# Exact 12-bit-part products from the first unit of the second batch on, in a fused sketch attention and SwiGLU kernel

## The chip, the cores and the metric

The kernel runs on one core of a Trainium2 chip. The metric is the device time of one execution in microseconds (us). Five engines work side by side, each through its own queue in order: TensorE (PE, with its weight loads shown as PEld), VectorE (DVE), ScalarE (ACT), GpSimd (POOL) and SyncE (SP), which issues most of the DMAs.

## The reference

There are 4 batches of 4 heads, 1088 positions and 32 channels. Queries and keys are projected by two 8 x 32 sketches, and the outer product of the two projections gives 64 features per position. The attention is linear: sums over the keys, then one quotient per query. Its output, 4352 tokens of 128 channels, goes through a SwiGLU block with 1536 hidden channels.

```python
def phi(x):
    a = np.einsum('rd,bhsd->bhsr', S1, x)
    b = np.einsum('rd,bhsd->bhsr', S2, x)
    return np.einsum('bhsi,bhsj->bhsij', a, b).reshape(*x.shape[:-1], r * r)
kv = np.einsum('bhsf,bhsd->bhfd', k_p, v);  z = np.sum(k_p, axis=2)
num = np.einsum('bhsf,bhfd->bhsd', q_p, kv)
den = np.einsum('bhsf,bhf->bhs', q_p, z)[..., None] + 1e-06
x = (num / den)                       # regrouped to (tokens, 128)
g = x @ w_gate;  silu = g * (1.0 / (1.0 + np.exp(-g)))
out = (silu * (x @ w_val)) @ w_out
```

The sketches and the three weights come as 64-bit floats and are narrowed to fp32 in the kernel.

## The kernel before, in words

**The SwiGLU work.** Each batch is cut into three blocks of tokens, of 384, 384 and 320. The hidden channels are cut into 12 chunks of 128. A *unit* (i, j) is the gate and the value product of block i with chunk j, the SiLU, and the product of the two, which goes to a slot of hbuf. A *down* (L936) multiplies such a slot with w_out and adds to the block's accumulator, a PSUM bank called acc. Batch 0 is handled by a loop over z (30 units, after six that are written out by hand). Then all downs of batch 0 that are left run in a row. Batches 1 to 3 are one loop over y = 0 to 107 (L1177), nine blocks of 12 units: y 0 to 35 is batch 1, y 36 to 71 batch 2, the rest batch 3. After each unit one down runs, which lags some units behind.

**Two kinds of products.** A plain unit (L903) makes both products in fp32: two matmul instructions each. A cut unit (L868) makes the value product, or with both=True both products, of fp32r parts that are exact in few bits. The weights are cut into w1, wb and wd (L835), the tokens into x1, x0 and xd (L850). A cut product is wd.xd in one bank (L877), and w1.x1 + wb.x0 in another (L883, L884). ScalarE scales the first into a tile called sum (L889). VectorE adds the second from PSUM to it (scalar_tensor_tensor, L892). In a cut unit the last product, SiLU times value, runs on GpSimd (L901); in a plain unit it runs on VectorE (L928). Cutting a token block takes one ScalarE pass (L858), a difference (L859) and a VectorE pass (L863). The plain units are y < 38; y 38 to 47 cut the value product; from y = 48 on both are cut; y = 107 is plain. The value weights are cut at y 2 to 21, the gate weights at y 14 to 33, with differences and wd on GpSimd (L838).

**The attention of the next batches** is a generator, attentions (L563). parts_of (L1087) advances it a step or two after each unit; group (L1093) runs it up to the next yield "pe", and then does the TensorE work behind it. Most of its steps are VectorE instructions: features (L355), transposes (L305, L540), the denominators (L719 to L741), the features of the queries (L355) and their transposes phT (L750). The TensorE work is numerators (L760, matmuls L770, copies into xT L787), values (L674, matmuls L366 and L678), which needs the feature sums zs that GpSimd adds up (L521), and the sketches (L332, L320). spread_out (L683) then issues six DMAs and the loads of the next values. The groups stand at y = 12, 36 and 60. The group at 12 does the last two thirds of batch 1's numerators and the values and sketches of batch 2.

**PSUM** has eight banks. Up to y = 36, units take turns over three of them (g0, g1, g2). After that, bank() (L110) hands out the bank that was touched longest ago among seven, without acc and without those that a group holds.

**Order.** Every engine runs its instructions in the order in which this code issues them. A matmul waits for its inputs and for its bank's last reader, and nothing behind it on TensorE passes it.

Of the kernel before, what the change touches and what calls it, by code (L numbers as in the profile page):

```python
# [19 lines left out]
def kernel(  # L20
# [265 lines left out]
    def run(*gens):  # L286
        for g in gens:
            for _ in g:
                pass
# [231 lines left out]
    def feature_sums(phk):  # L521

        rows = phk[:].rearrange("p c h i j -> p c (h i j)")
        s = apool.tile([P, 4, H * F], FP32, tag="zs", name="zs")
        add = lambda o, a, b: nc.gpsimd.tensor_tensor(out=o, in0=a, in1=b, op=ALU.add)  # L525
        add(s[:], rows[:, 0:4, :], rows[:, 4:8, :])
        add(s[:, 0:2, :], s[:, 0:2, :], s[:, 2:4, :])
        add(s[:, 0, :], s[:, 0, :], s[:, 1, :])
        add(s[:, 0, :], s[:, 0, :], rows[:, 8, :])
        return s[:, 0, :]  # L530

    def turns(b):

# [29 lines left out]
    def attentions():  # L563

        yield from turns(1)
        hold("a", "b")
        kp, qp = wide("a"), wide("b")
        for ps, products in ((kp, key_products), (qp, query_sketches)):
            for i, c in enumerate(kpieces):
                products(ps[:, i, :], *c)
        ka = apool.tile([P, NC * H, R], FP32, tag="kas", name="kas")
        qab = apool.tile([P, 2, NC * H, R], FP32, tag="qab", name="qab", bufs=2)
        fac = None, qab  # L580

        def sketch(ps, i):
            c0, c1 = kpieces[i]
            return ps[:, i, 0 : 64 * (c1 - c0)].rearrange("p (x t r) -> p x t r", t=2, r=R)

        for i, (c0, c1) in enumerate(kpieces):
            nc.scalar.copy(ka[:, H * c0 : H * c1, :], sketch(kp, i)[:, :, 0, :])
        phk = apool.tile([P, NC, H, R, R], FP32, tag="phk", name="phk")
        for n, (i, c0, c1) in enumerate(((0, 0, 3), (0, 3, 5), (1, 5, 7), (1, 7, 9))):
            first = H * (c0 - kpieces[i][0])  # L590
            kb = sketch(kp, i)[:, first : first + H * (c1 - c0), 1, :]
            key_features(phk, (ka[:, H * c0 : H * c1, :], kb), c0, c1)
            if n < 2:
                q0, q1 = kpieces[n]
                nc.scalar.copy(
                    qab[:, :, H * q0 : H * q1, :], sketch(qp, n).rearrange("p x t r -> p t x r")
                )
            if n == 1:
                release("b")
            if n == 3:  # L600
                release("a")
            if n % 3 != 1:
                yield
        zs = feature_sums(phk)
        for i, _ in enumerate(turns(2)):
            if i % 2:
                yield
        hold("a", "b")
        kvz = wide("a")
        values(kvz[:, 0, :], phk, zs)  # L610
        kq = wide("b")
        fac2, copies = sketches([
            (0, NC - 1, kq[:, 0], kq[:, 1]),
            (NC - 1, NC, kvz[:, 1, 0 : 2 * F], kvz[:, 1, 2 * F : 4 * F]),
        ])
        spread = spread_out(1, kvz[:, 0, :])
        for _ in range(4):
            yield
            run_copies(copies, 1)
        release("a", "b")  # L620
        step = query_step(1, fac, spread)
        yield from step(0, 3)
        numerators(1, spread, 0, 3)
        yield "first"
        yield from step(3, NC)
        phk = hbuf[:, NH - 6 :, :].rearrange("p s (n h i j) -> p (s n) h i j", h=1, i=R, j=R)
        phk = phk.rearrange("p (c h) o i j -> p c (h o) i j", h=H)
        yield from features(phk, fac2, ())
        zs = feature_sums(phk)
        yield from turns(3)  # L630
        yield "pe"
        numerators(1, spread, 3, NC)
        hold("a", "b")
        kv = bank()
        values(kv, phk, zs)
        kp, qp = wide("a"), wide("b")
        fac3, copies = sketches([(c0, c1, kp[:, i], qp[:, i]) for i, (c0, c1) in enumerate(kpieces)])
        spread = spread_out(2, kv)
        run_copies(copies, 2)
        yield  # L640
        run_copies(copies, 2)
        release("a", "b")
        yield
        yield from features(phk, fac3, ())
        zs = feature_sums(phk)
        yield from query_step(2, fac2, spread)(0, NC)
        yield "pe"
        numerators(2, spread, 0, NC)
        kv = bank()
        values(kv, phk, zs)  # L650
        spread = spread_out(3, kv)
        for _ in range(4):
            yield
        yield from query_step(3, fac3, spread)(0, NC)
        yield "pe"
        numerators(3, spread, 0, NC)
        yield

    def run_copies(copies, n):
        for f, *args in copies[:n]:  # L660
            f(*args)
        del copies[:n]
# [132 lines left out]

    LAG = 2
    hidden = {}
    acc = {}  # L800
    todo = []
# [14 lines left out]
    def whole(ap):  # L816
        return ap.bitcast(FP32)
# [14 lines left out]
                for k in range(2):  # L832
                    yield [x[:, k] for x in t]

    def cut_weights(w, at, steps):  # L835

        def put(at, f, **args):
            steps.setdefault(at, []).append(lambda: f(**args))  # L838

        for c, (w1, wb, wd) in enumerate(homes(w)):  # L840
            src = w[:, 3 * c : 3 * c + 3, :]
            low = fpool.tile([P, 3, P], FP32, tag="sgl", name="low", bufs=6)[:]
            w_parts[id(w), c] = (w1, wb, wd)
            sub = dict(op=ALU.subtract)
            put(at + c, nc.scalar.activation, out=w1, in_=src, func=AF.Copy, scale=CUT)
            put(at + 4 + c, nc.gpsimd.tensor_tensor, out=low, in0=src, in1=whole(w1), **sub)
            put(at + 12 + c, nc.scalar.activation, out=wb, in_=low, func=AF.Copy, scale=BETA)
            put(at + 16 + c, nc.gpsimd.tensor_tensor, out=wd, in0=whole(w1), in1=whole(wb), **sub)

    def cut_tokens(i, engine=nc.gpsimd):  # L850

# [16 lines left out]
    def cut_unit(i, j, both=False):  # L868
# [22 lines left out]
        for p, s in zip(ps, sums):  # L891
            nc.vector.scalar_tensor_tensor(  # L892
                out=s, in0=p, scalar=1.0 + 1.0 / BETA, in1=s, op0=ALU.mult, op1=ALU.add
            )
        sg = fpool.tile([P, BW], FP32, tag="sg", name="sg", bufs=3)[:, 0:n]
        nc.scalar.activation(sg, sums[0] if both else g, AF.Silu)  # L896
        slot_of[i, j] = slots.pop(0)
        hj = hbuf[:, slot_of[i, j], :]
# [4 lines left out]
    def unit(i, j, late=False, between=(None, None)):  # L903
# [4 lines left out]
        for o, w in ((g, wg), (u, wv)):  # L908
# [3 lines left out]
                o[:, 0:n], w[:, j, :], xT[:, t0 : t0 + n], start=True, stop=True  # L912
            )
        sg = fpool.tile(
            [P, BW], FP32, tag="sgl" if late else "sg", name="sg", bufs=6 if late else 3
        )
        nc.scalar.activation(sg[:, 0:n], g[:, 0:n], AF.Silu)  # L917
        slot_of[i, j] = slots.pop(0)
# [163 lines left out]


    att = attentions()
    ahead = [None]

    def parts_of(n):  # L1087

        for _ in range(n):
            if ahead[0] not in ("pe", "end"):  # L1090
                ahead[0] = next(att, "end")

    def group():  # L1093
        while ahead[0] != "pe":
# [45 lines left out]
    for z, (i, j) in enumerate(seq):  # L1140
        if z == 17:
            free_banks.pop()
            turn[0] %= 4
        unit(i, j)
        for p in parts.get(z, ()):
            part(*p)
        if z in (24, 25, 26):
            catch_up()
        if z == 6:
            load_k(1)  # L1150
            load_v(1, [nc.sync] * 4)
            load_q(1)
        if z >= 17:
            todo.remove(order[0])
            todo.insert(0, order.pop(0))
            down()
        if z >= 17:
            parts_of(1)
    todo.sort()
    while todo:  # L1160
        for _ in range(min(3, len(todo))):
            down()
        if ahead[0] != "first":
            parts_of(1)
    while ahead[0] != "first":
        parts_of(1)

    slots[:] = range(NH - 6)

    line = [3 * b + k for b in range(1, B) for k in ((0, 2, 1) if b == B - 1 else range(3))]
    END = len(line) * NCH
    PLAIN, VALUE = 3 * NCH + 2, 4 * NCH
    coming_x = iter(())
    cutting = {}
    for y in range(END):  # L1177
        i, j = line[y // NCH], y % NCH
        if y in (NCH, 3 * NCH, 5 * NCH):
            group()  # L1180
        if y == 3 * NCH:
            oldest[0] = True
            hold("acc")
            run(cut_tokens(i, nc.vector))
        if y < PLAIN or y == END - 1:
            unit(i, j)
        else:
            cut_unit(i, j, both=y >= VALUE)
        lag = LAG if y < PLAIN else min(5, END - y + 1)
        for _ in range(2):  # L1190
            if len(todo) > lag:
                down()
        parts_of(2 if y in (0, 4, 6, 7, 8) else 1)
        for w, at in ((wv, 2), (wg, 14)):
            if y == at:
                cut_weights(w, at, cutting)
        for step in cutting.pop(y, ()):
            step()
        if j == 4 and 3 * NCH < y < END - NCH:
            coming_x = cut_tokens(line[y // NCH + 1])  # L1200
        if j in (4, 6):
            next(coming_x, None)
    ps = wide("a")[:, 0, 0:D]
    for j in range(NCH):
        if todo and j % 4 == 0:
# [40 lines left out]
```

## Time and profile before

| what | value |
|---|---|
| 8 runs, median (lowest to highest) | 292.91 us (292.09 to 293.52) |
| the profiled execution's own time | 292.41 us |
| its span from first to last instruction | 290.7 us |
| around the span | 1.7 us |
| granted TensorE clock | 1.00 in the whole span |
| batch 0's last unit ends, downs in a row | 77.35 to 92.6 us |
| y = 0 starts | 92.6 us |
| numerators of the groups at y = 12, 36, 60 start | 114.6, 163.0, 206.8 us |
| L892, L889, L901 (cut units) | 526, 465, 1016 ns each |
| L928, L917 (plain units) | 524, 474 ns each |
| L525 (feature sums) on 128x1024, 128x512, 128x256 | 2362, 1470, 729 ns each |

The profile lists for each engine its busy time, and for each group of equal instructions the number, the mean duration and what the engine waited for. A matmul's end is modelled, so the distance from one start to the next on TensorE says more than the duration. The chain of waits lists the work that led to the end, in order of time: start, duration, what ran. The timeline lists instructions of an engine with the idle time before them in brackets.

### The profile page before, as it was taken

How to read it: one execution, taken by the hardware profiler on the slowest of the kernel's cores; microseconds unless marked ns; L12 is line 12 of the kernel's file. 1: busy time of each engine (PE TensorE's matmuls, PEld its weight loads, DVE VectorE, ACT ScalarE, POOL GpSimd, SP SyncE). 2: the span in 40 equal slices, each digit the busy share in tenths (PEclk: the TensorE clock that was granted, in tenths of full speed). 3: DMA queues.
4: the chain of work that ended last, by engine and by line, in shares of the span. 5: the costliest groups of instructions: out<-in, count | busy, mean ns of one | idle time of the engine just before them, and what ended most of it. 6: DMA issues, size and time to landing. Idle time of an engine off the chain costs nothing.

```text
span 290.7 us, 6170 instructions
## 1 busy us (share of the span) xinstructions
PE 283.9 (98%) x2307; PEld 204.3 (70%) x2307; DVE 200.8 (69%) x400; ACT 154.6 (53%) x369; POOL 130.2 (45%) x144
## 2 busy tenths in 40 slices
PE   7899999999999999999999999999999999999995
PEld 7545566667666555755667677778788988888985
DVE  3997988875542997188893369997567675676651
ACT  3567565431301432353243365578688888888860
POOL 3215322138000308029741039676466676576660
PEclk9999999999999999999999999999999999999999
DMA  6564292315511100140010020001001010020101
GB/s 198 153 213 110 64 302 82 99 59 162 118 16 27 17 0 2 36 102 0 0 28 3 2 50 0 2 0 27 2 1 28 2 23 0 0 32 0 24 2 27
DMA packets 26142, 14.63 MB, mean 50 GB/s; under 512 B 18688, under 2 KB 24192, under 8 KB 26112
## 3 DMA queue, kind: packets, MB, share of 16 engines
q1 hardware_dynamic: 25456, 14.13, 19.3%
q8 instruction: 18, 0.29, 0.4%
q10 hardware_dynamic: 656, 0.10, 0.2%
q14 instruction: 12, 0.10, 0.1%
HBM read 11.41 MB, written 2.23 MB: 47 GB/s over the span
## 4 chain that ended last, share of the span: by engine, by line
PE 91%; DVE 3%; DMA 1%; issue 1%; ACT 1%; POOL 0%; SPq 0%; DVEq 0%
PE PS L911 32%; PE PS L942 28%; PE PS L877 7%; PE PS L883 7%; PE PS L884 7%; PE PS L879 2%; PE PS L770 2%; PE PS L332 2%; PE PS L366 2%; DMA kld<-in_k_dram 1%; PE PS L320 1%; DVE sum L892 1%; PE PS L957 1%; PE PS L475 1%; PE PS L423 1%
## 5 line engine op out<-in xcount | busy, mean ns | idle before, releaser
L942 PE MATMUL PS<-hbuf,wo 128*128 128x384 f32 (+2 forms) x288 | 104.7, 460 | 0.4 <-DVE o L971 0.4
L901 POOL TENSOR_TENSOR hbuf<-sg,sum 128x384 f32<-128x384 f32 (+1 forms) x69 | 69.9, 1016 | 53.6 <-ACT sg L896 31.3
L892 DVE SCALAR_TENSOR_TENSOR sum<-PS,sum 128x384 f32<-128x384 f32 (+1 forms) x128 | 62.6, 526 | 29.5 <-ACT sum L889 27.2
L917 ACT ACTIVATE sg<-PS 128x384 f32<-128x384 f32 (+1 forms) x75 | 35.4, 474 | 68.5 <-PE PS L911 66.1
L942 PEld LDWEIGHTS PS<-hbuf,wo 128*128 128x128 f32 x288 | 52.5, 189 | 17.6 <-issue 0.7
L911 PE MATMUL PS<-xT,wg 128*128 128x384 f32 (+1 forms) x150 | 59.1, 476 | 0.0
L911 PE MATMUL PS<-xT,wv 128*128 128x384 f32 (+1 forms) x150 | 58.2, 470 | 0.2 <-DVE wv L270 0.2
L889 ACT ACTIVATE sum<-PS 128x384 f32<-128x384 f32 (+1 forms) x128 | 53.4, 465 | 5.6 <-PE PS L877 5.2
L928 DVE TENSOR_TENSOR hbuf<-sg,PS 128x384 f32<-128x384 f32 (+1 forms) x69 | 36.1, 524 | 28.6 <-PE PS L911 26.8
L911 PEld LDWEIGHTS PS<-xT,wv 128*128 128x128 f32 x150 | 28.2, 190 | 18.0 <-DVE hbuf L928 0.9
L911 PEld LDWEIGHTS PS<-xT,wg 128*128 128x128 f32 x150 | 27.6, 190 | 18.2 <-issue 1.2
L896 ACT ACTIVATE sg<-sum 128x384 f32<-128x384 f32 (+1 forms) x59 | 29.7, 503 | 17.1 <-DVE sum L892 16.4
L877 PE MATMUL PS<-xd,gphq 128*128 128x384 f32 (+1 forms) x59 | 34.6, 587 | 0.0
L883 PE MATMUL PS<-x,w 128*128 128x384 f32 (+1 forms) x69 | 25.4, 368 | 0.0
L877 PE MATMUL PS<-xd,wd 128*128 128x384 f32 (+1 forms) x69 | 24.6, 357 | 0.0
L884 PE MATMUL PS<-x,wb 128*128 128x384 f32 (+1 forms) x69 | 22.6, 328 | 0.0
L883 PE MATMUL PS<-x,graw 128*128 128x384 f32 (+1 forms) x59 | 19.2, 325 | 0.0
L884 PE MATMUL PS<-x,graw 128*128 128x384 f32 (+1 forms) x59 | 19.1, 324 | 0.0
L877 PEld LDWEIGHTS PS<-xd,wd 128*128 128x128 f32 x69 | 13.1, 189 | 6.8
L838 POOL TENSOR_TENSOR low<-wv,w 128x384 f32<-128x384 f32 x4 | 4.7, 1175 | 25.4 <-ACT w L838 25.4
L877 PEld LDWEIGHTS PS<-xd,gphq 128*128 128x128 f32 x59 | 11.1, 189 | 6.4 <-issue 0.4
L525 POOL TENSOR_TENSOR zs<-hbuf 128x1024 f32<-128x1024 f32 x2 | 4.7, 2362 | 21.5 <-PE PS L911 11.7
(129 smaller groups left out, 339.9 us busy)
## 6 DMA issues: line engine op xcount, KB each, us to landing
kld<-in_k_dram SPq DMA_DIRECT2D x4, 544.0 KB, 4.3
vld<-in_v_dram SPq DMA_DIRECT2D x12, 144.0 KB, 5.4
qld<-in_q_dram SPq DMA_DIRECT2D x3, 544.0 KB, 4.3
raw<-in_moe_w_out_dram SPq DMA_DIRECT2D x4, 384.0 KB, 4.1
out_dram<-o SPq DMA_DIRECT2D x28, 48.0 KB, 1.9
raw<-in_moe_w_gate_dram SPq DMA_DIRECT2D x3, 384.0 KB, 3.3
raw<-in_moe_w_val_dram SPq DMA_DIRECT2D x3, 384.0 KB, 3.3
out_dram<-o SPq DMA_DIRECT2D x16, 40.0 KB, 1.7
```

Source lines behind the costliest of these rows:

```text
L332: nc.tensor.matmul(ps[32 * a : 32 * a + 64, 64 * (c - c0) : 64 * (c - c0) + 64], kT[:, c, a : a + 2, :].rearrange("p a t -> p (a t)"), s12 ...
L877: nc.tensor.matmul(d, wd, xd, start=True, stop=True)
L883: nc.tensor.matmul(p, w1, x1, start=True, stop=False)
L884: nc.tensor.matmul(p, wb, x0, start=False, stop=True)
L889: nc.scalar.activation(s, d, AF.Copy, scale=-1.0 / BETA)
L892: nc.vector.scalar_tensor_tensor(out=s, in0=p, scalar=1.0 + 1.0 / BETA, in1=s, op0=ALU.mult, op1=ALU.add)
L896: nc.scalar.activation(sg, sums[0] if both else g, AF.Silu)
L901: nc.gpsimd.tensor_tensor(out=hj[:, 0:n], in0=sg, in1=sums[-1], op=ALU.mult)
L911: nc.tensor.matmul(o[:, 0:n], w[:, j, :], xT[:, t0 : t0 + n], start=True, stop=True)
L917: nc.scalar.activation(sg[:, 0:n], g[:, 0:n], AF.Silu)
L928: nc.vector.tensor_tensor(out=hj[:, 0:n], in0=sg[:, 0:n], in1=u[:, 0:n], op=ALU.mult)
L942: nc.tensor.matmul(acc[i][:, 0:n], wo[:, j, :], hidden[i, j][:, 0:n], start=(j == 0), stop=(j == NCH - 1),)
```

## The change

1. **Units.** All units y 0 to 106 are cut: the value product alone for y < 31, both from y = 31 on (GATES). The downs lag five units in all three batches. The rotation over seven banks begins at y = 0.
2. **Value weights** are cut in batch 0's loop, z = 24 to 29, with the differences on VectorE (z = 27). The first token block is cut during the row of downs, on VectorE; the differences of blocks 2 and 4 of the nine are on VectorE too.
3. **Gate weights** are cut from y = 8 to 28, the differences on VectorE; the tiles for them are four slots of hbuf, so the loop starts with 17 slots and not 21.
4. **Groups** stand at y = 7, 16, 34 and 64. The numerators of batch 1's last two thirds become a group of their own (y = 7), values and sketches of batch 2 follow at y = 16.
5. **Attention steps** run ahead in the row of downs: two at a time, and on after the first numerators ("turned", begun). From y = 36 on one step per two units. The feature sums of batches 2 and 3 are five GpSimd adds, spread over four steps of what runs beside them. The four copies of the sketches run in one go.

```diff
     def feature_sums(phk):
-        add(s[:], rows[:, 0:4, :], rows[:, 4:8, :])
-        add(s[:, 0:2, :], s[:, 0:2, :], s[:, 2:4, :])
-        add(s[:, 0, :], s[:, 0, :], s[:, 1, :])
-        add(s[:, 0, :], s[:, 0, :], rows[:, 8, :])
-        return s[:, 0, :]
+        def last():
+            add(s[:, 0, :], s[:, 0, :], s[:, 1, :])
+            add(s[:, 0, :], s[:, 0, :], rows[:, 8, :])
+        return s[:, 0, :], [
+            lambda: add(s[:, 0:2, :], rows[:, 0:2, :], rows[:, 4:6, :]),
+            lambda: add(s[:, 2:4, :], rows[:, 2:4, :], rows[:, 6:8, :]),
+            lambda: add(s[:, 0:2, :], s[:, 0:2, :], s[:, 2:4, :]),
+            last,
+        ]
+    def beside(gen, steps):
+        for x in gen:
+            if steps:
+                steps.pop(0)()
+            yield x
...
         yield from step(0, 3)
+        yield "turned"
         numerators(1, spread, 0, 3)
         yield "first"
         yield from step(3, NC)
+        yield "pe"
+        numerators(1, spread, 3, NC)
+        yield
...
-        zs = feature_sums(phk)
-        yield from turns(3)
+        zs, sums = feature_sums(phk)
+        yield from beside(turns(3), sums)
         yield "pe"
-        numerators(1, spread, 3, NC)
...
-        run_copies(copies, 2)
-        yield
-        run_copies(copies, 2)
+        run_copies(copies, 4)
...
+    def take(steps, n):
+        for _ in range(n):
+            if steps:
+                f, args = steps.pop(0)
+                f(**args)
...
+        if z == 24:
+            lows = [fpool.tile([P, 3, P], FP32, tag="sgl", name="low", bufs=6)[:] for c in range(4)]
+            first, low, second, third = cut_weights(wv, [(nc.vector, low) for low in lows])
+        if z in (25, 26):
+            take(first, 2)
+        if z == 27:
+            take(low, 4)
+        if z > 27:
+            take(second, 2)
+            take(third, 2)
...
-        if ahead[0] != "first":
-            parts_of(1)
-    while ahead[0] != "first":
+        if begun[0]:
+            x_steps = x_steps or cut_tokens(HEAD, nc.vector)
+            next(x_steps, None)
+        parts_of(1 if begun[0] or ahead[0] == "turned" else 2)
+    while not begun[0]:
         parts_of(1)
-    slots[:] = range(NH - 6)
+    run(x_steps or cut_tokens(HEAD, nc.vector))
+    slots[:] = range(NH - 10)
...
-    PLAIN, VALUE = 3 * NCH + 2, 4 * NCH
+    GROUPS, GATES = (7, 16, 34, 64), 31
+    for m, i in enumerate(line[1:], 1):
+        gen = cut_tokens(i, nc.vector if m in (1, 3) else nc.gpsimd)
+        for at in {1: (8, 9), 3: (34, 35), 6: (65, 69)}.get(m, (NCH * m - 9, NCH * m - 4)):
+            token_steps.setdefault(at, []).append(gen)
+    oldest[0] = True
+    hold("acc")
+    lows = [hbuf[:, NH - 10 + c, :].rearrange("p (c f) -> p c f", f=P) for c in range(4)]
     for y in range(END):
-        if y in (NCH, 3 * NCH, 5 * NCH):
+        if y in GROUPS:
             group()
-        if y < PLAIN or y == END - 1:
+        if y == END - 1:
             unit(i, j)
         else:
-            cut_unit(i, j, both=y >= VALUE)
-        lag = LAG if y < PLAIN else min(5, END - y + 1)
+            cut_unit(i, j, both=y >= GATES)
-        parts_of(2 if y in (0, 4, 6, 7, 8) else 1)
+        parts_of(y < 36 or y % 2)
+        if y == 8:
+            gate_rows = cut_weights(wg, [(nc.vector, low) for low in lows])
+        for n, row in enumerate(gate_rows):
+            if y >= (8, 12, 16, 22)[n] and (n < 3 or y % 2 == 0):
+                take(row, 1)
+        for gen in token_steps.get(y, ()):
+            next(gen, None)
```

cut_weights returns its four rows of steps (w1, difference, wb, wd) instead of placing them by unit; the tiles sg have five buffers instead of three.

## The prediction

> **What bounds the kernel now.** I read the page's busy row and slices first, then the chain of waits, then the VectorE and GpSimd timelines at the places where the change puts work.
>
> ```profile
> PE 283.9 (98%) x2307; PEld 204.3 (70%) x2307; DVE 200.8 (69%) x400; ACT 154.6 (53%) x369; POOL 130.2 (45%) x144
> ...
> DVE  3997988875542997188893369997567675676651
> ...
> POOL 3215322138000308029741039676466676576660
> PEclk9999999999999999999999999999999999999999
> ...
> PE 91%; DVE 3%; DMA 1%; issue 1%; ACT 1%; POOL 0%; SPq 0%; DVEq 0%
> ```
>
> TensorE works all the time at full clock and makes 91% of the chain, so its instruction stream is the time. VectorE is the next limit: in slices 14 to 21 (about 92 to 152 us, batch 1) it is mostly at 7 to 9 tenths, where GpSimd is nearly idle until 128 us.
>
> The price of a unit is the distance between two downs (L942) in the chain of waits.
>
> ```profile
> 100.45 0.65 PE PS L942 x2
> 101.10 1.29 PE PS L911 x4
> 102.39 0.65 PE PS L942 x2
> ...
> 157.57 0.54 PE PS L942 x2
> 158.11 1.08 PE PS L911 x4
> 159.19 0.54 PE PS L942 x2
> ...
> 177.87 0.65 PE PS L942 x2
> ...
> 179.68 0.65 PE PS L942 x2
> ...
> 199.37 0.65 PE PS L942 x2
> ...
> 201.06 0.65 PE PS L942 x2
> ...
> 220.40 0.54 PE PS L942 x2
> ...
> 221.81 0.54 PE PS L942 x2
> ```
>
> At 384 tokens: plain 1.94 us, value product cut 1.81, both cut 1.69. At 320: plain 1.62, both 1.41. The value-only unit at 320 is not in the trace; it lies between 1.62 and 1.41, and I take the middle, 1.52.
>
> **What TensorE saves.**
> - y 0 to 23, plain to value-only at 384: 24 x 0.125 = 3.0 us (exact periods over runs of units: 1.935 and 1.813, so 2.9).
> - y 24 to 30, the same at 320: 7 x 0.10 = 0.7 (bounds 0 and 1.4).
> - y 31 to 35, plain to both at 320: 5 x 0.20 = 1.0.
> - y 36 and 37, plain to both at 384: 2 x 0.25 = 0.5.
> - y 38 to 47, value-only to both at 384: 10 x 0.12 = 1.2.
>
> Together 6.3 us, between 5.6 and 7.0. The downs, numerators, values and sketches have the same matmuls as before, in another order.
>
> **What moves to the other engines.** The instruction order of the changed program shows 107 cut units against 69. A value-only unit costs VectorE what a plain one did (L892 526 ns for L928 524), ScalarE one L889 more (465 ns, at 53% busy) and GpSimd one L901 (1.0 us per 1.8 us). GpSimd takes that easily by itself. VectorE gets in batch 1 what it did not have: four gate differences and two token differences (0.56 each, by L859) and three xd passes (L863, 0.5 to 0.6), some 5 us in 70. The weight differences at z = 27 fall into idle time (VectorE waits 3.2 us before 74.0). They push the following steps by some 0.6 us; the first numerators are reached by TensorE after 13 downs, at 85.6, and phT would be ready near 83.8, because the output transpose that VectorE waits 4.0 us for at 85.1 now stands behind it. Eleven downs (5.9 us) then cover cutting the first token block (ScalarE 0.5, VectorE 0.6 and 0.6, and a 0.95 us product between them): ready near 89.9, needed at 92.5. I cost the start of batch 1 at nothing; without this cover it would be those 2.7 us.
>
> **What TensorE will wait for.** I laid the VectorE order of the new program against the units' times above, with spacings from the timeline (768-element passes 0.86 to 0.99, L892 0.47, the denominators 2.35 in all).
> - *Group at y = 7.* TensorE arrives after seven units without and two downs, 92.5 + 9.5 = 102.0. VectorE has seven L892 (3.3), five transposes and passes of step(3, NC) and the denominators, 10.1 us in all and first work at 92.6: phT near 102, banks free near 102.8. Wait 0.9 (bounds 0 and 2).
> - *Group at y = 16.* The sums are five adds between the hidden products of y 10 to 13: 3 x 1.35 + 2 x 0.75 = 5.5 us (1.35 is the undisturbed spacing of the 128x512 add at 112.2 in GpSimd's timeline) more in units that give GpSimd 7.3 us and take 4 of it. zs ends some 11.3 us after y = 10's products, and the ones-product needs it at 10.6. With a collision, 0.8 (0 to 2). In exchange the 0.46 us hole at 119.2, where TensorE waits in the sketches, goes.
> - *Batch 1's end.* From y = 26 on the denominators, and then a query feature pass (L355) or a phT pass per unit of 1.4 to 1.6 us, put VectorE about 1 us behind. The output transpose of block 4 and the group at y = 34 then come late: 0.6 (0 to 1.5).
> - *y = 36.* Before, the group at 36 cut its block at once, and two plain units covered it:
>
> ```profile
> 165.88 0.53 ACT L858 ACTIVATE x<-xT 128x384 fp32r<-128x384 f32 x1
> 166.44 0.56 DVE L859 TENSOR_TENSOR x<-xT,x 128x384 fp32r<-128x384 f32 x1 [0.17 <-ACT x L858]
> 167.04 0.56 DVE L863 SCALAR_TENSOR_TENSOR xd<-x,x 128x384 fp32r<-128x384 f32 x1
> ```
>
> Now the difference is issued after unit 34 and xd after unit 35, behind both of its L892. These cannot start before unit 35's last product, 0.54 us before unit 36; the pair takes 0.93, xd 0.56, so xd is at least 0.9 us late, and the first matmul of unit 36 is wd.xd. With ScalarE's queue (x1 stands between the copies of units 34 and 35) I get 1.4 (0.9 to 2).
> - *y = 52, 53.* The denominators of batch 3 (2.35) now stand ahead of unit 52's L892 pair and the output transpose that frees acc. By the units' period that is 1.0 late (0 to 1.5). Before, the same wait stood at 195.0, with 0.62 in front of L942; that one goes.
>
> Waits added 4.7, gone 1.1: 3.6 net. Nothing queued behind these waits can pass, on TensorE, so they count in full. SP only gets the spread and value loads of batch 2 four units later; its reader L719 stands four units behind the group, 7.3 us against 6 x 0.6 of issues and a landing like the one before 77.9, which was 2.5 behind its last issue.
>
> Sum: 6.3 - 3.6 = 2.7 us less. From the profiled 292.41 (span 290.7 and 1.7 around it) that is 289.7; the median of the runs is 0.5 higher, and I forecast for it 290.0, between the two readings 289.7 and 290.2.
>
> **The shared port.** The row that speaks against the change is this one, VectorE's first product of batch 3 and what GpSimd did then:
>
> ```profile
> 129.75 2.07 DVE L719 TENSOR_TENSOR phq<-spread,qab 128x768 f32<-128x768 f32 x1
> ...
> 133.62 0.95 DVE L719 TENSOR_TENSOR phq<-spread,qab 128x768 f32<-128x768 f32 x1
> ```
>
> ```profile
> 128.65 2.36 POOL L525 TENSOR_TENSOR zs<-hbuf 128x1024 f32<-128x1024 f32 x1 [11.68 <-PE PS L911]
> 131.08 2.68 POOL L525 TENSOR_TENSOR zs<-zs 128x512 f32<-128x512 f32 x2
> ```
>
> The first one took 1.1 us more than the second, and it ends 0.8 to 0.9 us (its normal length) after GpSimd's add. L892, which reads one input from PSUM, keeps its 0.55 us throughout. The Trainium skill, in "SBUF — State Buffer", in the section that tells engine ports from DMA ports, says that a VectorE instruction with two SBUF inputs and a GpSimd instruction exclude each other for the whole instruction, whoever is first. By that rule, each such VectorE instruction in batch 1 waits up to the whole GpSimd instruction that it meets; for 25 of them at 1.0 us it would be 25 us of VectorE time, and the change a loss. The trace is milder: nine L719 average 1159 ns over a median of 951, 0.2 us each, and nine L355 (phq) 1023 over 942, 0.1 each. My waits hold 0.2 to 0.3 for some of them.
>
> **The rivals.**
> 1. *Clean* (0.17). The waits are covered by the banks' slack, because every short wait lets VectorE catch up: then 6.3 less, and some of the 1.1 gone too. For it: before, VectorE at 9 tenths in slices 14, 15 and 17 to 21 stalled TensorE only at groups. Against: the wait at y = 36 is forced. 286.0 to 287.6.
> 2. *Eaten* (0.17). The five waits each reach their upper bound, 9.0 instead of 4.7: gain 6.3 - 7.9 = -1.6; half of the way there is 291.5 to 293.5, of which I give 0.10 to still faster and 0.07 to no change.
> 3. *Slower* (0.13): the port between VectorE and GpSimd. Between y = 0 and 33 VectorE gets 25 instructions with two SBUF inputs (L719, L355, L741, the differences), all now beside a GpSimd that works half the time or more: 4 up to y = 6, where VectorE has no slack, 9 up to y = 15 with 4.3 us of slack (13.3 us of work in 17.6), 12 up to y = 33 with 3.5 (26.5 in 30). At 0.55 each (half an L901): 2.2 + 0.7 + 3.1 = 6.0 more, and 295 to 296. It decides from about 0.42 each (1.7 + 0 + 1.5 = 3.2, which eats the 2.7). For it: between 129 and 152 us, where GpSimd was busy, eight such instructions lost 1.1, 0, 0.4, 0.1, 0.3, 0, 0 and 0.8, 0.33 on average. Against: the averages above.
> 4. That the change doesn't do what it says is excluded by the order: the units and groups stand where the text puts them.
>
> **How the numbers follow.** The forecast's case, 287.6 to 291.5, has 0.53. Its own bounds come from the waits: 0.9 (only the forced one) gives 286.5, all upper ones 294. Faster by over 0.2% (0.6 us, about what a measurement of this kernel can tell from no change): 0.53 + 0.17 + 0.10 = 0.80; within: 0.07; slower: 0.13. The range leaves out the slower case and most of no change, and the low end of the clean one: 286.4 to 292.6.
>
> **What would show it.** Right: down-to-down distances of 1.81 in y 6 to 15 and of 1.69 from y = 36; idle TensorE in front of L786 (numerators) near 102, and 0.9 to 2 in front of the first wd.xd of unit 36; VectorE above 8 tenths in batch 1. Wrong: L735 or L355 averaging over 1.4 us (rival 3); value-only units longer than 1.85; a wait of several us in front of the ones-product at y = 16; or none at y = 36.

## The result: slower by 1.5%

The changed kernel takes 296.8 us (median of 11 runs, 296.2 to 298.3), the kernel before 292.77 (32 runs, 292.08 to 293.52). The ratio is 1.0154, with a 95% interval of 1.0140 to 1.0167. The forecast was a faster kernel, 290.0 (286.4 to 292.6). The changed kernel's times lie at two levels: 296.2 to 296.8 where the granted clock is 0.998 or more, and 298.0 to 298.3 where it is 0.992 to 0.994. The profiled execution (298.18, span 296.4) is of the second; the half clock, below, makes the levels.

The page of the changed kernel: the busy row, three rows of slices, the chain's shares.

```profile
PE 282.3 (95%) x2362; PEld 211.9 (71%) x2362; DVE 218.3 (74%) x430; ACT 179.8 (61%) x427; POOL 165.8 (56%) x178
...
DVE  3997988873967879359996578898866666576651
...
POOL 3216322156601858938999367656647675666660
PEclk9999999999999999989999999999999999999999
...
PE 77%; POOL 9%; DVE 6%; issue 4%; DMA 1%; ACT 1%; SPq 0%; POOLq 0%; ACTq 0%; DVEq 0%
```

TensorE fell from 98% to 95% busy and from 91% to 77% of the chain. GpSimd, which had 0% of the chain, has 9%: in slice 17 (119 to 126 us) and slices 19 to 22 (133 to 163 us) it is nearly full. The waits of TensorE from 92 us on say where (us in total, times, longest):

```profile
PE PS L694 <- POOL zs L525: 2.0, 1, 2.0
PE PS L906 <- DVE xd L892: 1.7, 1, 1.7
PE PS L971 <- DVE o L1000: 1.3, 1, 1.3
PE PS L906 <- POOL gphq L877: 1.2, 2, 1.0
PE PS L786 <- DVE phT L766: 1.0, 1, 1.0
PE PS L971 <- POOL hbuf L930: 0.9, 1, 0.9
```

(L694 is the ones-product, L906 wd.xd, L971 the down, L786 the numerators.) The kernel before had 0.7 there in all. As distances between matmul starts beyond the matmul's own length, which are a little longer, the waits are: y = 16 2.23 (ones-product); y = 28 to 33 1.03, 1.13 and 0.42 (down, and wd.xd for the gate weights); y = 36 1.82; y = 52 and 53 1.50 (in front of the down behind unit 53); y = 64 1.17.

The account of the profiled execution: by the units' periods TensorE's work is 6.3 us less, yet the span is 5.7 longer (296.4 against 290.7), so 12.0 went elsewhere. Found are 9.3 in these seven waits, less 1.1 that the kernel before had; 1.6 at half clock behind the first of them; 0.5 in the numerators at y = 34 (1.94 against 1.48 in the chains of waits; I read it as PSUM banks that came free late, which is not shown); 0.6 with those at y = 7 (2.16 from the down ahead of them to the matmul behind them, where the same numerators took 1.59 before). That is 10.9. Of the other 1.1, 0.3 stand in front of a down at 178.3 us and 0.4 lie in y 72 to 107 (55.80 against 55.36 us), with no single wait to name; the rest I can't place.

**The half clock.** TensorE's timeline of the changed kernel, and its windows (busy times, then the granted clock):

```profile
123.72 0.32 PE L694 MATMUL PS<-zs,ones 128*32 128x64 f32 x8 [2.04 <-POOL zs L525]
...
125.29 2.15 PE L320 MATMUL PS<-s,qT 128*32 128x64 f32 x72
```

```profile
120.50:125.00 4.50, 2.46 (x115) 2.21 (x116) 1.08 (x3) 0.39 (x2) 4.42 (x6) 1.00 0.01 4
125.00:128.40 3.40, 3.40 (x84) 2.91 (x79) 0.00 (x0) 1.73 (x5) 1.42 (x2) 0.50 0.16 39
128.40:135.00 6.60, 6.60 (x28) 4.69 (x26) 5.58 (x8) 4.90 (x12) 2.33 (x2) 1.00 0.58 129
```

After 2.04 us without work the clock is 0.50 for 3.4 us, which costs about half of that: the 1.6 us between the levels. The idle time of 1.7 us at y = 36 has no such sequel.

### The profile page after: what moved, and what is told of

Read it like the earlier page. It is cut to its first block, busy times and chain, and to the rows that moved or that the text cites. A ratio compares the mean times of both kernels' runs of the same rounds, so it can differ in the third digit from the quotient of the medians.

```text
span 296.4 us, 6492 instructions
## 1 busy us (share of the span) xinstructions
PE 282.3 (95%) x2362; PEld 211.9 (71%) x2362; DVE 218.3 (74%) x430; ACT 179.8 (61%) x427; POOL 165.8 (56%) x178
## 3 DMA queue, kind: packets, MB, share of 16 engines
HBM read 11.41 MB, written 2.23 MB: 46 GB/s over the span
## 4 chain that ended last, share of the span: by engine, by line
PE 77%; POOL 9%; DVE 6%; issue 4%; DMA 1%; ACT 1%; SPq 0%; POOLq 0%; ACTq 0%; DVEq 0%
PE PS L971 24%; PE PS L940 15%; PE PS L906 9%; PE PS L912 8%; PE PS L913 8%; POOL hbuf L930 4%; POOL zs L525 4%; PE PS L908 3%; PE PS L786 2%; DVE sum L921 2%; PE PS L332 2%; DMA kld<-in_k_dram 1%; PE PS L320 1%; PE PS L366 1%; PE PS L986 1%
## 5 line engine op out<-in xcount | busy, mean ns | idle before, releaser
L930 POOL TENSOR_TENSOR hbuf<-sg,sum 128x384 f32<-128x384 f32 (+1 forms) x107 | 113.3, 1064 | 72.8 <-ACT sg L925 46.4
L921 DVE SCALAR_TENSOR_TENSOR sum<-PS,sum 128x384 f32<-128x384 f32 (+1 forms) x183 | 89.8, 525 | 38.3 <-ACT sum L918 30.2
L971 PE MATMUL PS<-hbuf,wo 128*128 128x384 f32 (+2 forms) x288 | 105.0, 461 | 2.4 <-DVE o L1000 1.3
L918 ACT ACTIVATE sum<-PS 128x384 f32<-128x384 f32 (+1 forms) x183 | 77.7, 467 | 20.6 <-PE PS L906 18.9
L971 PEld LDWEIGHTS PS<-hbuf,wo 128*128 128x128 f32 x288 | 51.4, 188 | 12.3 <-issue 2.3
L906 PE MATMUL PS<-xd,gphq 128*128 128x384 f32 (+1 forms) x76 | 44.1, 580 | 2.9 <-DVE xd L892 1.7
L912 PE MATMUL PS<-x,w 128*128 128x384 f32 (+1 forms) x107 | 43.6, 407 | 0.0
L906 PE MATMUL PS<-xd,wd 128*128 128x384 f32 (+1 forms) x107 | 42.6, 398 | 0.0
L946 ACT ACTIVATE sg<-PS 128x384 f32<-128x384 f32 (+1 forms) x37 | 17.4, 474 | 21.2 <-PE PS L940 19.6
L940 PE MATMUL PS<-xT,wv 128*128 128x384 f32 (+1 forms) x74 | 28.8, 471 | 0.2 <-DVE wv L270 0.2
L906 PEld LDWEIGHTS PS<-xd,wd 128*128 128x128 f32 x107 | 20.4, 190 | 10.9 <-issue 0.4
L957 DVE TENSOR_TENSOR hbuf<-sg,PS 128x384 f32<-128x384 f32 (+1 forms) x31 | 16.2, 524 | 10.0 <-PE PS L940 9.5
L912 PEld LDWEIGHTS PS<-x,w 128*128 128x128 f32 x107 | 20.2, 188 | 4.1 <-ACT xT L803 0.3
L906 PEld LDWEIGHTS PS<-xd,gphq 128*128 128x128 f32 x76 | 14.3, 189 | 12.2 <-POOL gphq L877 2.2
L913 PEld LDWEIGHTS PS<-x,wb 128*128 128x128 f32 x107 | 20.1, 188 | 3.7
```

The costliest lines, as they stand in the source:

```text
L906: nc.tensor.matmul(d, wd, xd, start=True, stop=True)
L912: nc.tensor.matmul(p, w1, x1, start=True, stop=False)
L913: nc.tensor.matmul(p, wb, x0, start=False, stop=True)
L918: nc.scalar.activation(s, d, AF.Copy, scale=-1.0 / BETA)
L921: nc.vector.scalar_tensor_tensor(out=s, in0=p, scalar=1.0 + 1.0 / BETA, in1=s, op0=ALU.mult, op1=ALU.add)
L930: nc.gpsimd.tensor_tensor(out=hj[:, 0:n], in0=sg, in1=sums[-1], op=ALU.mult)
```

## The experiments

First theory: GpSimd's queue makes the waits from y = 16 to 33, and four orders of VectorE's work (token parts, denominators, phT, banks) those from y = 34 on. Rival: VectorE, or its port shared with GpSimd, makes them all. The kernels ran in four groups, each beside the kernel before (medians 292.6 to 292.7). "Waits" are the distances defined above.

**The sums together** (295.39, 295.22 to 295.48; ratio 1.0091, 1.0074 to 1.0108; clock 1.0)

```
-        yield from beside(turns(3), sums)
+        for f in sums:
+            f()
+        yield from turns(3)
```

and the same beside query_step(2, ...).

> The feature sums of batches 2 and 3 are issued in one go ahead of the turns and query steps, not spread between GpSimd's hidden products; nothing else differs from the changed kernel. If GpSimd's queue order holds TensorE up at y = 16 (wait of 2.0 us in front of the ones-product, then 3.4 us at half clock), the wait and the half clock go: 2.2 + 1.7 us less than the profiled 298.2, so 294 to 295 us, and the waits at y = 28 to 33 stay (2.6 us) because GpSimd has the same work. If VectorE is what is late (rival), the ones-product was waiting for features, not for the adds behind hidden products, and the time stays at 296 to 298.

The wait in front of the ones-product goes. In the sketches behind it 0.79 are left, where the kernel before had 0.46 and the forecast had counted on none. No half clock follows: 1.4 us under the median, 1.1 under the executions at full clock, and 0.4 above the range that was expected. At y = 25 to 33 2.7 us of waits stay (0.74 of them now name VectorE's output transpose), so the spread of the sums is not what makes those.

**The wait filled** with 20 useless matmuls of 256 columns ahead of the ones-product (297.11, 296.87 to 297.81; ratio 1.0153, 1.0136 to 1.017; clock 0.999 to 1.0)

```
+        if begun[0] and not warmed:
+            warmed.append(1)
+            keep_warm(20, 256, ps=kv[:, 256:512])
...
+    warmed = []
```

> Twenty matmuls of 256 columns without a use (about 2.1 us at full clock) are put between the value products and the ones-product of the group at y = 16, in unused columns of the same bank. If the half clock behind that group comes from TensorE's idle 2 us, the granted clock stays 1.00 and every run is at the lower of the two levels of the changed kernel, 296.2 to 296.8 (the upper one is 298.0 to 298.3). If the clock drops for another reason, the two levels stay, or the time grows by up to 2 us.

No execution has the half clock, and y 16 to 23 take 14.32 us where the changed kernel's profile has 14.80. The time is 0.3 above the range that was expected; y = 0 begins 1.2 us later in this profile, which I can't explain. So it is idleness that brings the half clock (by four executions here; the last section counts all), and filling it without ending the wait gains nothing at the median.

**Block 3's token parts at y = 34** (296.75, 295.18 to 296.9; ratio 1.0124, 1.0097 to 1.0152)

```
+        if y == 34:
+            run(token_steps.pop(34)[0])
+            token_steps.pop(35)
```

> The block of y = 36 is cut at once in the group at y = 34, ahead of unit 34, not in two steps behind units 34 and 35. If the wait of 1.8 us in front of the first product of unit 36 comes from VectorE's order (the step of the forecast), it goes and the time falls by 1.5 to 1.8 us. If VectorE is simply late there, or the wait only moves into unit 34 (its sums stand behind the cut), it falls by less than 0.7.

The wait of 1.82 at y = 36 goes, but one of 0.83 comes in front of a down at 175.7. At equal clock the gain is 1.3 (295.18 against 296.5 at full clock, 296.8 against 298.1 at the lower), between the theory's 1.5 to 1.8 and the rival's 0.7.

**Plain units up to y = 23** (294.86, 294.48 to 295.16; ratio 1.0071, 1.0056 to 1.0086; clock 1.0)

```
-        if y == END - 1:
+        if y < 24 or y == END - 1:
```

> Units y = 0 to 23 are plain, as before the change; the rest of the change stays. TensorE's products cost 24 x 0.12 = 2.9 us more, and GpSimd loses 24 hidden products (24 us of its queue). If GpSimd is the bound up to y = 33, the waits at y = 16 and y = 28 to 33 (2.2 and 2.6 us) and the half clock (1.7 in the profiled run) go: net 1.9 to 3.6 us less than the changed kernel. If VectorE is the bound, its work is the same (a product for a sum), the waits stay and the time is 1 to 3 us more.

All waits that name GpSimd go, at y = 16 as at 28 to 33, and the half clock; those at y = 36, 53 and 64 stay at 1.82, 1.50 and 1.17. Although TensorE has 3.0 us more to do, the time is 1.9 less. The next runs turned to y 34 to 64.

**One attention step per unit** from y = 36 on too (298.42, 298.3 to 299.75; ratio 1.0206, 1.0177 to 1.0235)

```
-        parts_of(y < 36 or y % 2)
+        parts_of(1)
```

> The changed kernel with one attention step per unit from y = 36 on too, where the changed kernel takes one per two units. Theory of the late orders: the 1.17 us in front of the group at y = 64 goes (phT is ready units earlier), the 1.50 at y = 52 and 53 stays or moves with its denominators, the waits at y = 16, 28 to 33 and 36 stay: 295.0 to 296.5. Rival (VectorE itself is short of time from y = 36 on, so the pace is not what makes phT late): waits of the same 1.2 us or more come back in front of other units of y 36 to 60, and the time stays at 296.5 or rises.

The wait at y = 64 goes as the theory said, but new ones of 0.70, 0.53 and 1.16 come between 176 and 189 us and the one of 1.50 behind unit 53 is still 1.20: the rival. VectorE is busy 24.81 of the 25 us from 170 to 195.

**One part alone, in the kernel before:** the gates cut from y = 38 on (296.29, 296.02 to 296.39; ratio 1.0121, 1.0101 to 1.0141; clock 1.0)

```
-    PLAIN, VALUE = 3 * NCH + 2, 4 * NCH
+    PLAIN, VALUE = 3 * NCH + 2, 3 * NCH + 2
```

> The kernel before with one part of the change alone: the gate weights cut from y = 38 on instead of y = 48; plain units, sums, groups and numerators as before. Ten units at 1.69 instead of 1.81 us are 1.2 us less TensorE time. Theory (the TensorE savings are right, and what eats them is GpSimd in y 10 to 33 and four late orders): 291.4 to 291.9, the whole 1.2 or nearly. Rival (cut gates cost more than their periods show, by the port between VectorE's xd and GpSimd): 292.5 or more, with waits in front of units of y 38 to 47.

Here my theory of late orders fell. Ten units get 0.12 us shorter on TensorE each, no order is touched, and the kernel is 3.7 us slower. VectorE's timeline, first in the kernel before and then in this one, tells why:

```profile
178.76 1.29 DVE L719 TENSOR_TENSOR phq<-spread,qab 128x768 f32<-128x768 f32 x1
179.97 0.55 DVE L892 SCALAR_TENSOR_TENSOR sum<-PS,sum 128x384 f32<-128x384 f32 x1
180.43 0.94 DVE L726 TENSOR_REDUCE dot<-phq 128x96 f32<-128x768 f32 x1
181.60 0.56 DVE L892 SCALAR_TENSOR_TENSOR sum<-PS,sum 128x384 f32<-128x384 f32 x1 [0.23 <-PE PS L884]
```

```profile
182.38 1.01 DVE L892 SCALAR_TENSOR_TENSOR sum<-PS,sum 128x384 f32<-128x384 f32 x2
183.32 0.94 DVE L726 TENSOR_REDUCE dot<-phq 128x96 f32<-128x768 f32 x1
184.18 1.00 DVE L892 SCALAR_TENSOR_TENSOR sum<-PS,sum 128x384 f32<-128x384 f32 x2
185.10 0.44 DVE L735 TENSOR_TENSOR dot<-dot,qab 128x288 f32<-128x288 f32 x1
```

In the first, the unit's sum takes 0.46 us (179.97 to 180.43) and the step beside it 0.94, 1.40 of a period of 1.81, and VectorE idles 0.23. In the second the unit has two sums (x2): 0.94 from 182.38 to 183.32, and 0.86 for the step, 1.80 where TensorE's period is 1.69. The pairs now follow each other at VectorE's 1.8 us, there is no gap to catch up in, and the sums and the output transposes then come late. TensorE's waits in this run:

```profile
PE PS L942 <- DVE o L971: 1.3, 1, 1.3
PE PS L877 <- DVE sum L892: 0.9, 2, 0.7
```

**The orders mended** in the changed kernel (296.47, 295.95 to 296.83; ratio 1.0126, 1.0099 to 1.0153): the sums together and block 3's parts at y = 34, as above, and

```
-    GROUPS, GATES = (7, 16, 34, 64), 31
+    GROUPS, GATES = (7, 16, 34, 67), 31
...
-        parts_of(y < 36 or y % 2)
+        parts_of(y < 36 or y % 2 == 0)
```

with block 6 cut at y = 68 and 70 where it was 65 and 69.

> The changed kernel with its orders mended and its units as they are: the sums together ahead of the products beside them, block 3's token difference and xd at y = 34, the attention steps on the even units from y = 36, the last group at y = 67. From the run with the sums together (295.4): the waits of 1.94 (y = 36) and 1.34 (y = 64) go, the 1.5 at y = 52 falls to some 0.6; what is left is GpSimd's 3.8 us of waits in y 16 to 33. Theory: 291.0 to 292.0. Rival (VectorE is short as a whole, and mending one order makes the next one late): 293.5 to 295.4.

The waits at y = 36 and in front of the last group are gone, and others stand at 173 (1.11), 194 (0.64), 196 (1.19), 206 (0.66) and 218 us (1.06). It is even 1.1 us slower than the sums together alone: every mended order made the next thing late. That was the rival's sign, and worse than its number.

**The same with y 16 to 23 plain** (294.71, 294.51 to 295.26; ratio 1.0072, 1.005 to 1.0094)

```
-        if y == END - 1:
+        if 16 <= y < 24 or y == END - 1:
```

> The same with the units y 16 to 23 plain. It costs TensorE 8 x 0.12 = 1.0 us and takes 8 hidden products of 1.0 to 1.15 us from GpSimd. Theory (GpSimd's queue makes the waits of y 16 to 33): those 3.8 us go nearly whole, and the time is 2 to 3 us under that of the mended orders alone: 288.5 to 290. Rival (the waits there are VectorE's, which has the same work in a plain unit): only the 1.0 us is seen, and the time is 0 to 1 us above that of the mended orders alone.

The 2.7 us of waits from 142 to 157 us go nearly whole; less the 1.0 of TensorE that leaves 1.7, and 1.8 was measured, just under the theory's 2 to 3. A plain unit has as much VectorE work as the value-only one, so this is GpSimd: from 142 to 156 us VectorE is busy 13.13 of 14 us here and 13.65 in the run above, GpSimd 12.15 and 14.00. The time is above 290 because the waits from 171 us on stay (five of 0.6 to 1.2).

**Gates from y = 48 on, as before, one step per unit** (295.5, 295.24 to 297.07; ratio 1.0108, 1.0076 to 1.0139; half clock in all executions)

```
-    GROUPS, GATES = (7, 16, 34, 64), 31
+    GROUPS, GATES = (7, 16, 34, 64), 48
...
-        parts_of(y < 36 or y % 2)
+        parts_of(1)
```

> The changed kernel with its gates cut from y = 48 on, as in the kernel before, and one attention step per unit throughout; the value products stay cut from y = 0. TensorE gives back 2.0 us (5 x 0.11 and 12 x 0.12). Theory (a unit with both products cut takes two sums of 0.50 us from VectorE where the other takes one, which leaves too little of a 1.69 us period for an attention step of 0.9): of the 5.4 us of waits from y = 34 on, 3.5 to 4.5 go, and the time is 294.2 to 295.3. Rival (those waits come from the order of the instructions and not from VectorE's load): the waits at y = 36, 52 and 64 stay, and the time is 298 to 299.

From y = 34 on, only 0.86 (y = 36) and 0.79 (y = 53) remain of waits over 0.4. Taken at equal clock (295.5 against 298.1) the time is 2.6 less (0.2 above the theory's range), although TensorE has 2.0 more to do: the cut gates of y 31 to 47 and their pace cost 4.6, of which 1.5 are the waits at y = 31 and 33 for the gate weights' wd, which name GpSimd.

**Both mends: gates from 48, sums together, block 3's parts at 34, y 16 to 23 plain** (291.04, 290.94 to 291.24; ratio 0.9945, 0.9924 to 0.9966; clock 1.0). Edits: those of the runs above (the groups stay at 7, 16, 34 and 64).

> Gates cut from y = 48 on and one step per unit as in the run beside it, and with it the sums together, block 3's token parts at y = 34, and y 16 to 23 plain. Both theories together (GpSimd in y 10 to 33, VectorE from y = 34): 3.2 us of TensorE time saved against before (y 0 to 15, 24 to 35, 36 and 37), and waits of 1.2 left in place of 1.1: 289.5 to 291, faster than before. Rival (each mended wait comes back as another): 292.5 to 294.5.

The first version under both kernels, at the upper end of what was expected. Of waits over 0.3 there are left 0.79 in the sketches at y = 16, 0.31 at y = 34 and 0.78 at y = 53.

**VectorE's load taken away** by leaving most of the gate's sum out, so that the output is another (296.77, 296.66 to 298.19; ratio 1.0151, 1.0122 to 1.018; half clock in all)

```
+            w = 32 if light and s is sums[0] else n
             nc.vector.scalar_tensor_tensor(
-                out=s, in0=p, ...
+                out=s[:, 0:w], in0=p[:, 0:w], ...
...
+            cut_unit(i, j, both=y >= GATES, light=GATES <= y < 60)
```

> The changed kernel, where VectorE adds the gate's main product in units y 31 to 59 for 32 of its columns alone (the rest of the gate keeps only the small part, so the output is another): 29 instructions of VectorE shrink from about 0.5 to 0.1 or 0.2 us, TensorE's work and all orders stay. Theory (VectorE's load makes the waits from y = 34 on): the late numerators at y = 34, the waits at 52 and 64 go and the one at 36 falls by half: 293.0 to 294.5. Rival (the orders alone): 296 to 297.

The time lies in the rival's range. At equal clock it is 1.4 us less than the changed kernel's (296.7 against 298.1). The waits at y = 36 and 53 fall to 1.34 and 1.03, that at y = 64 stays (1.15). By itself the load explains less than half.

**The differences on GpSimd** instead of VectorE (296.45, 296.34 to 296.5; ratio 1.0128, 1.0111 to 1.0146; clock 1.0)

```
-        gen = cut_tokens(i, nc.vector if m in (1, 3) else nc.gpsimd)
+        gen = cut_tokens(i, nc.vector if m == 3 else nc.gpsimd)
...
-            gate_rows = cut_weights(wg, [(nc.vector, low) for low in lows])
+            gate_rows = cut_weights(wg, [(nc.gpsimd, low) for low in lows])
```

> The changed kernel with the differences of the gate weights' four parts and of block 1's tokens on GpSimd instead of VectorE. VectorE gets some 2.8 us less and GpSimd some 3 to 5 us more between y = 8 and 27. Theory (GpSimd's queue makes the waits of y 10 to 33): longer waits at y = 16 and 28 to 33, 298.5 to 301. Rival (VectorE and the port it shares with GpSimd make them): 294 to 296.5.

The theory's 298.5 to 301 did not come, and the upper end of the rival's range is no gain: as fast as the changed kernel at full clock. GpSimd got some 5 us more work, yet zs came 0.4 sooner. GpSimd's timeline of the changed kernel, then of this one:

```profile
115.52 1.00 POOL L930 TENSOR_TENSOR hbuf<-sg,sum 128x384 f32<-128x384 f32 x1
116.48 1.60 POOL L525 TENSOR_TENSOR zs<-hbuf 128x512 f32<-128x512 f32 x1
118.04 1.32 POOL L930 TENSOR_TENSOR hbuf<-sg,sum 128x384 f32<-128x384 f32 x1
119.32 1.60 POOL L525 TENSOR_TENSOR zs<-zs 128x512 f32<-128x512 f32 x1
```

```profile
115.24 1.00 POOL L930 TENSOR_TENSOR hbuf<-sg,sum 128x384 f32<-128x384 f32 x1
116.21 1.27 POOL L525 TENSOR_TENSOR zs<-hbuf 128x512 f32<-128x512 f32 x1
117.45 1.00 POOL L930 TENSOR_TENSOR hbuf<-sg,sum 128x384 f32<-128x384 f32 x1
118.41 1.27 POOL L525 TENSOR_TENSOR zs<-zs 128x512 f32<-128x512 f32 x1
```

Without VectorE's differences beside them (L877, at 116 to 121 us) the sums take 1.27 instead of 1.60, and a product 1.00 instead of 1.32. So part of GpSimd's shortage is the port. VectorE pays there too: these four differences took 0.77 on average, where one of that size took 0.56 in the kernel before (L859). The rest of the added work fell into 125 to 135 us, where GpSimd had been busy 3.74 of 10 and now 8.84, and the waits at y = 28 to 33 didn't change (1.08, 1.13, 0.43). I had not looked for that gap.

**Load and pace together:** the light gate sum and one step per unit (294.35, 293.53 to 296.52; ratio 1.0054, 1.0026 to 1.0083)

> VectorE's gate sum of units y 31 to 59 over 32 columns alone, as in the run before (so the output is another), and one attention step per unit from y = 36 on. Theory (VectorE's load and the pace are one cause: the load is what makes the faster pace dear, and the slower pace is what makes the steps at y = 52 and 64 late): without the load the faster pace costs nothing, the waits at y = 64 (1.31) and most of that at 52 (1.04) go, and none comes back in y 38 to 50: 294.8 to 295.9. Rival (the faster pace is dear by itself, by the port or by the order): 297.5 to 299, as with the faster pace alone.

293.5 to 293.7 at full clock, 295.05 to 295.7 (and one 296.5) at the lower: 2.7 to 2.9 under the changed kernel at equal clock. The waits, first with the pace alone, then with pace and light sum:

```profile
PE PS L694 <- POOL zs L525: 2.0, 1, 2.0
PE PS L906 <- DVE xd L892: 1.7, 1, 1.7
PE PS L971 <- DVE o L1000: 1.6, 2, 1.0
PE PS L906 <- POOL gphq L877: 1.2, 2, 1.0
PE PS L971 <- POOL hbuf L930: 0.8, 1, 0.8
PE PS L906 <- DVE sum L921: 0.7, 1, 0.7
```

```profile
PE PS L694 <- POOL zs L525: 2.0, 1, 2.0
PE PS L906 <- POOL gphq L877: 1.2, 2, 1.0
PE PS L906 <- DVE xd L892: 1.2, 1, 1.2
PE PS L973 <- POOL hbuf L932: 0.8, 1, 0.8
```

No wait on o, phT or a sum is left. From y = 36 to 64 TensorE takes 50.84 us in the changed kernel, 52.70 with the pace alone, 50.03 with the light sum alone, 48.34 with both. Load and pace are one cause: the load leaves no room for a step per unit, and a step per two units makes denominators and phT late. A unit with both products cut also takes four of the seven banks where a value-only one takes three; with the light sum it still does, so the number of banks is not the cause.

**Four products given back to GpSimd:** the mended version with y 20 to 23 plain alone (290.66, 290.27 to 291.94; ratio 0.9930, 0.9912 to 0.9948; clock 1.0)

```
-        if 16 <= y < 24 or y == END - 1:
+        if 20 <= y < 24 or y == END - 1:
```

> The mended version (gates from y = 48, sums together, token parts at y = 34, one step per unit) with y 20 to 23 plain alone, where it had y 16 to 23: four more hidden products on GpSimd, which was idle for 8 of the 17 us from 125 to 142, and 0.5 us less TensorE time. Theory (GpSimd makes units wait only when its queue has no gap left): 290.3 to 290.8. Rival (every product there comes back as a wait): 291.0 to 292.0.

As the theory says, by the median; the intervals of this run and of the mended version overlap. No wait in its trace names GpSimd: where GpSimd's queue has gaps, a product there costs nothing. TensorE is at 98% again, and waits little:

```profile
PE 281.6 (98%) x2341; PEld 208.3 (72%) x2341; DVE 211.1 (73%) x413; ACT 172.5 (60%) x406; POOL 161.2 (56%) x174
```

```profile
PE PS L975 <- DVE o L1004: 1.0, 2, 0.6
PE PS L320 <- issue: 0.3, 1, 0.3
```

## Why the prediction was wrong

**TensorE's 6.3 us: right.** In the changed kernel's trace the starts of undisturbed units lie 1.81 us apart in y 8 to 14, 1.69 in y 43 to 51 and 1.41 in y 66 to 71. The value-only unit at 320, which was not in the trace, takes 1.62 with a down of 384 tokens behind it (y 24 to 27), and 1.51 with one of 320 (y 30 to 33 of the mended version with the gates from y = 48), for 1.52. **The start of batch 1 at nothing: right**; y = 0 starts at 92.36, before at 92.47. What failed is the other side of the sum: where it had 3.6 us of waits, net, the profiled execution has 12.0, 1.6 of them at half clock.

**"GpSimd takes that easily by itself": the step that failed first.** It set one product of 1.0 us against one unit of 1.8. The same queue has, beside the products, the second batch of sums and the four wd of the gate weights, which this step left out. Its reading that GpSimd is nearly idle until 128 us passes over slice 16 (109 to 116 us) of the row that it shows, where GpSimd stands at 8 tenths. GpSimd's share is the last busy time of the windows, in the kernel before and in the changed one:

```profile
112.00:125.00 13.00, 12.74 (x277) 8.58 (x276) 4.96 (x10) 3.86 (x11) 4.73 (x6) 1.00 0.19 50
...
135.00:160.00 25.00, 25.00 (x88) 16.44 (x88) 18.99 (x30) 7.98 (x18) 12.81 (x13) 1.00 0.06 9
```

```profile
112.00:125.00 13.00, 10.96 (x147) 7.91 (x148) 9.32 (x16) 5.76 (x14) 11.89 (x12) 1.00 0.00 1
...
135.00:160.00 25.00, 22.92 (x99) 16.44 (x98) 24.01 (x36) 12.96 (x29) 24.89 (x21) 1.00 0.06 9
```

12.81 of 25 became 24.89: some 14 of products, 6.95 of sums (1.27, 2.00, 2.00, 0.95, 0.73), 4.2 of wd. And the price was too low: the product took 1.15 us on average between 92 and 170 us, and sums 1.27 to 2.00, and the timelines above tie part of that to VectorE's instructions beside them. Runs with fewer products (plain units) remove exactly these waits.

**The group at y = 16: 0.8 (0 to 2), measured 2.23**, by the named mechanism, over its upper bound, and the half clock behind it (1.6 in about half of the executions) was not thought of. Of the four signs named for being wrong, "a wait of several us in front of the ones-product" is nearly this one.

**Batch 1's end: 0.6, put down to VectorE; measured 2.6 and 0.5.** The 2.6 name GpSimd, and go when it gets less; the 0.5 in the numerators name no engine.

**y = 36: 1.4 (0.9 to 2), measured 1.82: right**, mechanism and size; mending it gave 1.3. **y = 52, 53: 1.0, measured 1.50**, the forecast's upper bound. **y = 7: 0.9, measured 0.6.** **y = 64: not in the sum, 1.17**, from the pace, which the text had not priced.

**Gates cut from y = 31: the step that failed second.** 2.0 us of the 6.3 (5 x 0.11 at y 31 to 35, 12 x 0.12 at 36 to 47) were counted as gain because the units' periods on TensorE say so. Each costs VectorE 0.47 us more (two sums of 0.94 for one of 0.47), 8 us in 17 units, just where the attention steps of batch 3 make it the limit. The pair was in the text, but only as a delay at y = 36 and 52. One part alone in the kernel before cost 3.7 us where the same reasoning gave a gain of 1.2.

**Rival 3** named the right side and nearly the time (295 to 296), but its sign, L735 (the kernel before's L719) or L355 over 1.4 us on average, did not come: between 92 and 170 us L735 took 1.26 and L355 1.09. By my estimate from the means of both kernels there, VectorE's 25 instructions L735, L355, xd and differences lost some 7 us, 0.28 each, under the 0.42 from which rival 3 says that it decides. The price was largest on xd (1.03 on average for 0.56 before), which rival 3 did not list, and it fell on GpSimd as well. The Trainium skill ("SBUF — State Buffer", the section on SBUF's two sides) says that of a VectorE instruction with two SBUF inputs and a GpSimd instruction that reads SBUF, whichever starts first holds the pair of ports for its whole length and the other one blocks; in the pair of timelines above both lose (GpSimd 1.60 for 1.27, VectorE's differences 0.77 for 0.56), 0.2 to 0.3 us each and not a whole instruction. **Rival 1** read VectorE's row wrongly: of slices 17 to 21 the first is at 1 tenth and the next three at 8, not 9.

## To carry to other kernels

Before a step on the bounding engine is made shorter by giving work to others, add up for each stage everything that those engines' queues have there, and compare the sum per unit with the new, shorter period: 1.80 us of VectorE in a unit of 1.69 cost 3.7 us where 1.2 were to be gained. A pace of background work that is slowed so that it fits makes its results late, so load and pace must be tested together. A wait of 2 us on TensorE may cost more than its length.

## What the runs showed of the hardware that I had not expected

An idle time of 2.04 us, with only 32-column matmuls before it, brought TensorE to half clock for 3.4 us, in 6 of the 12 executions of the changed kernel (by their clock of 0.992 to 0.994) and in all four of the kernel with gates from y = 48. Over the six kernels with that gap (2.02 to 2.06 us in their traces) it came in 23 of 38 executions, and in none of four each where the gap was filled, where it was 1.61 us (the differences on GpSimd) and where the sums together ended it. In the run with the orders mended and the one with y 16 to 23 plain besides, whose longest idle times are about 1.0 us, one execution in four shows such a clock; where in the execution it stood is not on record. The Trainium skill ("TensorE: Matmul & The Clock Gate", "HAM oscillation") gives as its rule that no idle time of TensorE should exceed about 3.4 us; by that rule this gap was harmless. The measurement decides: 2.0 can be too much. Why one execution falls and the next doesn't, the traces suggest but don't prove. In every trace the clock, once up, changes only after a whole multiple of 3.41 us (here 119.47 us of full clock, 35 of them). In the five traces with the half clock, 1.87 to 2.05 us of the idle time lie within the one such stretch that ends where the clock drops; in the one trace that has the gap and keeps full clock (one attention step per unit), it falls on two of them, 1.17 and 0.88. So what counts seems to be how the gap falls on this grid, whose place differs from execution to execution.
